# A spectral and feed-forward network on one core: the second token transform in 64x64 tiles, with other load and instruction orders

## The chip, the cores and the metric

The kernel runs on one core of a Trainium2 chip. The metric is device time in microseconds, the median of several executions. One execution was also taken by the hardware profiler; its rows are quoted below. TensorE is called PE in the rows (its weight loads PEld), VectorE DVE, ScalarE ACT, GpSimd POOL and SyncE SP. The queues from which DMAs are issued are SP, ACT and POOL.

## What is computed

One sequence of S = 2048 tokens with D = 448 features passes through two spectral layers and two feed-forward layers in turn. All is bf16, with a residual added each time.

```python
def _A_ref(x, w_r, w_i):
    X = rfft2(x.astype(float32), axes=(-2, -1))
    X = X * (w_r + 1j * w_i)                       # [2048, 225]
    return irfft2(X, s=(S, D), axes=(-2, -1)).astype(bfloat16)

def _B_ref(x, w1, b1, w2, b2):                     # 448 -> 1792 -> 448
    h = relu(x @ w1 + b1) ** 2
    return h @ w2 + b2

for _ in range(2):
    x = x + _A_ref(_layernorm(x), w_r, w_i)
    x = x + _B_ref(_layernorm(x), w1, b1, w2, b2)
```

## The kernel before

The tokens are split as s = 16 p + t: p is the partition (128), t the tile (16 tiles of 128 x 448). The token transform of 2048 points is done in two steps, one over p (128 points) and one over t (16 points with twiddle factors), and the feature transform of 448 points lies between them. The stages of a spectral layer are:

- **A1** (first layer, `first_A`, line 871) or **A2** (second, `second_A`): for each tile t the transform over p. Mean and deviation come from VectorE (`ln_stats`) or, for tiles 1, 3 and 5, from ScalarE (`act_stats`). The matrix FA, scaled by 1/deviation (`scaled`, into Fs), is the moving operand of five matmuls per tile; the tile (xin) and its mirrored copy (xr, "XR", made by POOL or ScalarE, kept in VT's place) are the stationary ones. The result is evacuated to XA.
- **TD** (`stage_TD`, line 905): the feature transform. Sixteen numbers n, most taken in pairs; the columns of one n hold 4 frequencies x 16 tiles x 2 parts. It needs XA of all sixteen tiles. It is evacuated to U (in arena).
- **B** (`stage_B`, line 933): the 16-point transform over t. Each unit m0 (eight of them, 0 to 14 by two) takes 16 matmuls on 32x32 tiles of the array: four numbers n of one group G = m0 // 4 and two row strips. So a unit needs the U of four numbers n, that is of two TD pairs. It is evacuated to EF (in arena).
- **W** (`stage_W`, line 963): VectorE multiplies EF by the spectral weights Wt, into T3 (in wide). Wt holds rows of w_r and w_i that POOL gathers with indirect DMAs by the index tile ix.
- **Bi** (`stage_Bi`, line 968): eight products v of 32 matmuls on 64-row tiles, the inverse 16-point transform, evacuated to VT. Product v needs W of the numbers 2v and 2v+1.
- **TI** and **AI** (lines 994 and 1016): the inverse feature and token transforms per tile, added to x. TI needs all eight products.

The feed-forward layer follows with layer norm and transposes (`ln_B`), h (`h_part`, `h_pairs`) and o (`o_tile`).

PSUM is evacuated by ScalarE or VectorE; which of the two takes which tile is fixed by the order.

The order is written out by hand: `ORDER` (line 136) lists for each engine the numbers of the work units in the order in which it runs them. A planner (`_Sched.schedule`, line 369) goes through these lists with estimated costs, gives PSUM banks to the tiles, and puts filler matmuls (on `ones`, `warm_mm`, line 1340) into TensorE's gaps. It adds one where the planned gap is at least 120 ns and TensorE's planned work over a recent stretch is below the share `warm_share` (0.7). Every engine runs its list in order. `emit` (line 1349) writes the waits for an instruction's semaphores straight in front of it.

In the first layer TensorE's order after A1 is TD 0a, 0b, 1, 6, 7, 3; B 1, 7, 6; TD 2, 5, 4; B 2, 3, 4, 5, 0; then the products 2, 1, 4, 3, 7, 5, 0, 6 (numbers are pairs; pair 0 is cut into two single ones, and pairs 0 and 7 of B are evacuated in halves).

The loads of x: SP issues tile 0, then ix, FA, tiles 2-3, 6-7, 10-11 and 14-15; the ACT queue issues tile 1, then 4-5, 8-9 and 12-13. After them SP issues the matrices TD, G and G0 (for B), then, once tiles 10 to 13 have their deviations, H (for Bi), TI and the other weights. POOL issues six gathers: two for the first half of Wt (16 rows per partition), two of 15 rows and two of a single row for the second half. The single one is there because the mirrored list for the last strip of partitions holds the row of frequency 0 out of line.

Of the kernel before, what the change touches and what calls it, by code (L numbers as in the profile page):

```python
# [19 lines left out]
WS = 16 * (LW + 1) + 2  # L20
# [13 lines left out]
def make_constants():  # L34
# [45 lines left out]
    G = np.zeros((P, 16, 2, 32))  # L80
    G0 = np.zeros((P, 4, 32))
    for n in range(16):
        for i in range(4):
            C, Sn = wave(16 * (n % 4) + 4 * (n // 4) + i + 1)
            a, b = pair(C, Sn), pair(Sn, -C)
            G[32 * i:32 * i + 32, n] = np.stack([np.concatenate([a, -b], 1), np.concatenate([b, a], 1)], 1)
    z = np.zeros((16, 16))
    C, Sn = wave(64)
    for k, (a, b) in enumerate(((C, -Sn), (Sn, C))):
        G0[96:128, k] = np.concatenate([pair(a, z), pair(b, z)], 1)  # L90
    C, Sn = wave(0)
    for k, (a, b) in enumerate(((C, Sn), (-Sn, C))):
        G0[96:128, 2 + k] = np.concatenate([pair(z, a), pair(z, b)], 1)

# [23 lines left out]
    ix = np.stack([P * k + 16 * j + 1, P * (16 - k) - 16 * j - 15, np.where(j == 3, P * k, P * (16 - k) - 16 * j - 16)], 1)  # L118
# [28 lines left out]
1273 1234 1240 1278 1284 1281 1287 1290""",  # L147
    "act": """
# [11 lines left out]
1049 1229 1180 1182 1177 1175 1246 1244 1251 1256 1254 1261 1249 1264 1271 1269 1259 1266 1276 1274""",  # L160
    "dve": """
# [125 lines left out]
class _Sched:  # L287
# [6 lines left out]
    DMA_FIRST = 3500.0  # L294
    TURN = 100.0
    BEGIN = 800.0
    WINDOW = 3413.0

    def __init__(self):
        self.ops = {e: [] for e in self.ENGINES}  # L300
# [300 lines left out]
def bass_interleave_layers__spectral_gfnet__dense_activation_squared_relu__prompt_kernel(nc, A_x, A_w_r, A_w_i, B_x, B_w1, B_b1, B_w2, B_b2, out):  # L601
# [7 lines left out]
    with ExitStack() as es:  # L609
# [205 lines left out]
        for w in range(2):  # L815
            gather(2, w, WS * (2 + w), 1)
# [602 lines left out]
```

## Time and profile before

| | us |
|---|---|
| median of 3 runs | 262.47 |
| range of the runs | 262.4 to 263.34 |
| the profiled execution | 263.08 |
| its span, first to last instruction | 260.9 |
| TensorE busy (share of the span) | 248.7 (95%) |
| VectorE busy | 192.8 (74%) |
| ScalarE busy | 168.4 (65%) |
| POOL busy | 15.7 (6%) |

The profiled time lies 2.2 us above its span; what is outside the span is launch and end. A busy share is an average over stages with different limits: TensorE's 95% holds the feed-forward parts, where it never stops, and the spectral parts, where it does. Matmuls are pipelined, so the busy time of a single one counts its whole passage. The rows further below are read by stretches.

### The profile page before, as it was taken

The page shows a single profiled execution, that of the slowest core. Times are in us where ns is not written, and L with a number is a line of the kernel's source. Part 1 is how long each engine was busy: PE and PEld are TensorE (multiplying, and loading weights), DVE is VectorE, ACT ScalarE, POOL GpSimd, SP SyncE. Part 2 cuts the span into 40 slices and gives each one's busy share as a digit, 9 for nine tenths or more (in the row PEclk, how much of TensorE's full clock was granted, in tenths as well). Part 3 has the DMA queues.
Part 4 walks back from the last instruction along what each step waited for, and adds up shares of the span by engine and source line. Part 5 has one row for each costly group of instructions (what it writes and reads, how often), then busy time and mean ns, then how long its engine had stood idle before and what let it go on. Part 6 is the DMA issues. An engine that isn't in the chain of part 4 may idle for free.

```text
span 260.9 us, 6550 instructions
## 1 busy us (share of the span) xinstructions
PE 248.7 (95%) x2584; PEld 155.5 (60%) x2584; DVE 192.8 (74%) x625; ACT 168.4 (65%) x362; POOL 15.7 (6%) x31
## 2 busy tenths in 40 slices
PE   8799988999999989999998997999999999999996
PEld 2478687796544445554566666899554454544454
DVE  3985976889962999969999697899993359221562
ACT  6896985999238747306937897999557794007500
POOL 6791000000000000000000000000000000000000
PEclk9999997999999999999999999999999999999999
DMA  6989662111411000110000000020352001200025
GB/s 190 405 322 346 233 190 80 23 20 40 77 43 40 4 0 0 43 41 0 3 0 4 3 3 3 3 40 5 82 69 49 3 0 40 43 0 0 3 94 187
DMA packets 23789, 17.79 MB, mean 68 GB/s; under 512 B 16142, under 2 KB 22382, under 8 KB 23760
## 3 DMA queue, kind: packets, MB, share of 16 engines
q1 hardware_dynamic: 22544, 12.90, 18.6%
q0 software_dynamic: 640, 3.69, 3.5%
q10 hardware_dynamic: 576, 0.80, 1.0%
q8 instruction: 20, 0.33, 0.5%
q14 instruction: 9, 0.07, 0.1%
HBM read 11.88 MB, written 1.84 MB: 53 GB/s over the span
## 4 chain that ended last, share of the span: by engine, by line
PE 81%; DVE 9%; ACT 6%; DMA 2%; issue 1%; SPq 0%
PE ps L705 80%; ACT arena L730 3%; DVE arena L759 2%; DMA xin<-in_A_x_dram 2%; DVE st L835 1%; DVE XA L731 1%; DVE xin L759 1%; ACT wide L730 1%; DVE wide L759 1%; ACT VT L730 1%; ACT arena L724 0%; SPq L695 0%; DVE VT L1078 0%; PE ps L1341 0%; ACT mv L724 0%
## 5 line engine op out<-in xcount | busy, mean ns | idle before, releaser
L705 PE MATMUL ps<-wide,W_sb 64*128 64x512 bf16 (+1 forms) x770 | 90.0, 346 | 0.2 <-ACT wide L730 0.2
L705 PE MATMUL ps<-W_sb,arena 128*128 128x448 bf16 (+3 forms) x476 | 86.8, 342 | 0.0
L724 ACT ACTIVATE arena<-ps,b1col 128x512 bf16<-128x512 f32 x84 | 52.8, 687 | 32.1 <-PE ps L705 31.8
L705 PEld LDWEIGHTS ps<-wide,W_sb 64*128 64x128 bf16 (+1 forms) x770 | 50.8, 95 | 36.8 <-issue 1.7
L705 PEld LDWEIGHTS ps<-W_sb,arena 128*128 128x128 bf16 x476 | 45.5, 98 | 38.1 <-DVE arena L759 0.6
L759 DVE TENSOR_TENSOR arena<-arena 128x512 bf16<-128x512 bf16 (+1 forms) x140 | 45.0, 362 | 28.0 <-ACT arena L724 27.8
L730 ACT ACTIVATE arena<-ps 128x896 bf16<-128x896 f32 (+1 forms) x28 | 20.9, 850 | 3.4 <-PE ps L705 3.1
L724 ACT ACTIVATE mv<-mv,epst 128x1 f32<-128x1 f32 (+1 forms) x45 | 12.4, 292 | 13.1 <-DVE mv L768 7.0
L1077 ACT ACTIVATE VT<-x_sb 128x448 bf16<-128x448 bf16 x28 | 16.0, 575 | 7.1 <-DVE x_sb L1053 7.1
L724 ACT ACTIVATE arena<-ps 128x256 bf16<-128x256 f32 x56 | 17.4, 394 | 1.1 <-PE ps L705 1.0
L759 DVE TENSOR_TENSOR wide<-arena,Wt 128x896 bf16<-128x896 bf16 x32 | 17.7, 620 | 0.3 <-ACT arena L730 0.2
L705 PE MATMUL ps<-H_sb,wide 64*128 64x128 bf16 x512 | 16.4, 215 | 0.7 <-ACT arena L730 0.7
L705 PEld LDWEIGHTS ps<-H_sb,wide 64*128 64x128 bf16 x512 | 15.8, 94 | 2.0 <-DVE wide L759 1.3
L730 ACT ACTIVATE wide<-ps 128x896 bf16<-128x896 f32 (+3 forms) x20 | 14.4, 759 | 3.8 <-PE ps L705 3.5
L1199 DVE SCALAR_TENSOR_TENSOR x_sb<-ps,mv,xin 128x448 bf16<-128x448 f32 (+2 forms) x13 | 8.0, 644 | 11.4 <-PE ps L705 11.3
L705 PE MATMUL ps<-wide,VT 64*128 64x512 bf16 x42 | 15.8, 376 | 0.0
L730 ACT ACTIVATE XA<-ps 128x512 bf16<-128x512 f32 (+1 forms) x28 | 14.5, 591 | 1.3 <-PE ps L705 1.3
L730 ACT ACTIVATE VT<-ps 128x1024 bf16<-128x1024 f32 (+1 forms) x16 | 12.7, 829 | 2.7 <-PE ps L705 2.5
L705 PE MATMUL ps<-TI_sb,VT 112*128 112x112 bf16 (+1 forms) x128 | 10.7, 238 | 3.6 <-DVE VT L731 1.9
L741 ACT ACTIVATE wide<-x_sb,rstd 128x448 bf16<-128x448 bf16 x10 | 6.7, 668 | 9.2 <-DMA wide<-wide 7.9
L1053 DVE SCALAR_TENSOR_TENSOR x_sb<-ps,mv,xin 128x448 bf16<-128x448 f32 x16 | 10.8, 677 | 2.4 <-PE ps L705 2.3
L731 DVE CAST arena<-ps 128x896 bf16<-128x896 f32 (+1 forms) x10 | 8.2, 853 | 5.5 <-PE ps L705 5.5
(80 smaller groups left out, 279.7 us busy)
## 6 DMA issues: line engine op xcount, KB each, us to landing
out_dram<-x_sb SPq DMA_DIRECT2D x15, 112.0 KB, 1.8
W_sb<-in_B_w_dram SPq DMA_DIRECT2D x1, 1568.0 KB, 9.2
H_sb<-c_H SPq DMA_DIRECT2D x2, 768.0 KB, 10.2
W_sb<-in_B_w_dram SPq DMA_DIRECT2D x1, 1344.0 KB, 12.8
xin<-in_A_x_dram SPq DMA_DIRECT2D x4, 224.0 KB
xin<-in_A_x_dram ACTq DMA_DIRECT2D x3, 224.0 KB, 2.9
VT<-in_B_w_dram SPq DMA_DIRECT2D x2, 192.0 KB, 3.2
G_sb<-c_G SPq DMA_DIRECT2D x1, 256.0 KB
```

Source lines behind the costliest of these rows:

```text
L705: return sch.add("pe", lambda e: e.matmul(_res(o), lhsT, rhs, start=start, stop=stop, skip_group_check=skip), [lhsT, rhs], [o], cost=cost, ...
L724: sch.add("act", lambda e: e.activation(o, _res(i), func, **kw), rd, [o], cost=c)
L730: op = sch.add(engs[0], lambda e: e.activation(o, _res(i), ACT.Copy) if h[0].eng == "act" else e.tensor_copy(o, _res(i)), [i], [o], cost=c ...
L731: e.tensor_copy(o, _res(i)), [i], [o], cost=c[engs[0]], unit=unit)
L741: op = sch.add(engs[0], lambda e: e.activation(o, i, ACT.Copy, scale=s) if h[0].eng == "act" else e.tensor_scalar(o, i, s, 1.0, op0=ALU.mu ...
L759: sch.add(eng, lambda e: e.tensor_tensor(o, _res(a), b, op), [a, b], [o], cost=_free(o) / rate + 69.0)
L835: small(lambda e, si=si, xi=xi: e.bn_stats(si, xi), [xi], [si], _free(xi) / 0.96 + 69.0)
L1053: small(lambda e, xx=xx, xi=xi, r=r, m=m: e.scalar_tensor_tensor(out=xx, in0=_res(r), scalar=m, in1=xi, op0=ALU.subtract, op1=ALU.add), [r ...
L1077: op = sch.add("act", lambda e, i=i, o=o, x=x, h=h: e.activation(o, x, ACT.Square, accum_out=sd[:, i, 1:2]) if h[0].eng == "act" else e.sc ...
L1199: small(lambda e: e.scalar_tensor_tensor(out=o, in0=_res(i), scalar=rs[0] if rs else 1.0, in1=xi, op0=ALU.add if t >= 4 and last else ALU. ...
```

## The change

Stage B now runs on 64x64 tiles of the array: a unit m0 takes the numbers n = m0 and m0 + 1 alone, on two row halves. Two 32x32 matrices stand on the diagonal of each 64x64 matrix in G (and G0), and the rest of it is zero. For this FA takes the same order of frequencies as FI. G and G0 are twice as large. Since the zeros of the last number are in another strip now, the row of frequency 0 is loaded over the first row of the last 32 partitions by two plain DMAs on SP, after H; the gathers are four, of 16 rows each. Tiles 0 to 5 of x are loaded one by one. `emit` hangs TensorE's waits, but for the latest one of an instruction, on earlier instructions that have none. The planner's model of TensorE has a pace and depth of instruction supply (`PACE`, `DEEP`), and `warm_share` is 0.8. The orders of all engines are written anew; the order lists are left out here.

In the new order of the first layer TensorE runs, after A1, TD 3, 1, 7, 2, 6; B 7, 3, 1, 6; TD 4, 0a, 0b, 5; B 2, 4, 0; products 3, 7; B 5; products 1, 4, 0, 5, 2, 6. In the second it runs TD 7, 0b, 1, 4, 2, 5; B 7, 4, 2; TD 0a; B 1; TD 3; B 0, 5; product 7; B 3; TD 6; products 4, 0; B 6; products 2, 5, 1, 3, 6 (before: TD 7, 5, 6, 4, 1, 2, 0b, 0a; B 4, 7; TD 3; B 0, 1, 6, 5, 3; products 4, 7; B 2; products 0, 5, 3, 6, 1, 2). In A1 its tiles come as 0, 5, 1, 2, 3, 6, 7, 9, 8, 4, 12, 13, 10, 11, 14, 15 (before 1, 0, 4, 2, 3, 6, 7, 8, 9, 5, 13, 12, 10, 14, 11, 15). The ACT queue issues tile 1, 5, 8-9, 3, 12-13. POOL runs: ones, XR 0, XR 1, a memset, the scaling for tile 0, a gather of the second half, XR 4-5, XR 8-9, the scaling for tile 5, XR 2-3, XR 6-7, the other gather of the second half, XR 10-11, a scaling, a gather of the first half, XR 12-13, the last gather, XR 14-15, two scalings and two memsets.

```diff
-WS = 16 * (LW + 1) + 2
+WS = 16 * (LW + 1)
...
-            FA[:, n, i] = np.stack(comps(16 * (n % 4) + 4 * (n // 4) + i + 1), 1)
-            FI[n, i] = np.stack(comps(16 * (2 * (n % 2) + i % 2) + 2 * (n // 2) + i // 2 + 1), 0)
+            kappa = 16 * (2 * (n % 2) + i % 2) + 2 * (n // 2) + i // 2 + 1
+            FA[:, n, i] = np.stack(comps(kappa), 1)
+            FI[n, i] = np.stack(comps(kappa), 0)
...
-    G = np.zeros((P, 16, 2, 32))
-    G0 = np.zeros((P, 4, 32))
+    G = np.zeros((P, 16, 2, 64))
+    G0 = np.zeros((P, 4, 64))
...
+            r, c = slice(32 * i, 32 * i + 32), slice(32 * (i % 2), 32 * (i % 2) + 32)
+            G[r, n, :, c] = np.stack([np.concatenate([a, -b], 1), np.concatenate([b, a], 1)], 1)
...
-    ix = np.stack([P * k + 16 * j + 1, P * (16 - k) - 16 * j - 15, np.where(j == 3, P * k, P * (16 - k) - 16 * j - 16)], 1)
+    ix = np.stack([P * k + 16 * j + 1, P * (16 - k) - 16 * j - 16], 1)
...
-        self.warm_share = 0.7
+        self.warm_share = 0.8
...
+        def supply(start):
+            nonlocal sent
+            sent = max(sent + self.PACE, begun[-self.DEEP])
+            start = max(start, sent)
+            begun.append(start)
+            return start
...
-            a = WS * 2 + (LW + 1) * (15 - n) + (n < 15)
+            a = WS * 2 + (LW + 1) * (15 - n)
...
-        for i, (a, n) in enumerate(((0, 1), (1, 1), (2, 2), (4, 2), (6, 2), (8, 2), (10, 2), (12, 2), (14, 2))):
-            dma("act" if i % 2 else "sp", xin[:, a:a + n, :], x_dram[:, a:a + n, :])
-            if i == 0:
+        for a, n, q in ((0, 1, "sp"), (1, 1, "act"), (2, 1, "sp"), (3, 1, "act"), (4, 1, "sp"), (5, 1, "act"), (6, 2, "sp"),
+                        (8, 2, "act"), (10, 2, "sp"), (12, 2, "act"), (14, 2, "sp")):
+            dma(q, xin[:, a:a + n, :], x_dram[:, a:a + n, :])
+            if a == 2:
+                dma("sp", FA_sb[:], dc["FA"])
+            if a == 4:
                 dma("sp", ix[:], dc["ix"])
-                dma("sp", FA_sb[:], dc["FA"])
...
         for w in range(2):
-            gather(1, w, WS * (2 + w) + LW + 2, 15)
-        for w in range(2):
-            gather(2, w, WS * (2 + w), 1)
+            gather(1, w, WS * (2 + w), 16)
...
-            u = sch.new_unit("pe", 16, "q")
-            G, i0 = m0 // 4, m0 % 4
+            u = sch.new_unit("pe", 32, "quad")
             streams = []
-            for j in range(4):
+            for j in range(2):
                 for i in range(2):
-                    n, r = 4 * G + j, slice(32 * (i0 + i), 32 * (i0 + i) + 32)
+                    n, r = m0 + j, col(i)
...
-                    o = [lambda b, i=i, j=j, c=c: ps[32 * j:32 * j + 32, b + (i if both else 0), c] for c in
+                    o = [lambda b, i=i, j=j, c=c: ps[col(j), b + (i if both else 0), c] for c in
...
+        for w, a in enumerate((A_w_r, A_w_i)):
+            sch.tag = f"L.W0.{w}"
+            dma("sp", Wt[96:128, WS * (2 + w):WS * (2 + w) + LW + 1],
+                bass.AP(a.tensor, a.offset, [[0, 2], [P * (LW + 1), 16], [1, LW + 1]]))
...
+        def spread(ops, needs):
+
+            for i, op in enumerate(ops):
+                for key in sorted(needs[i], key=lambda k: needs[i][k][1])[:-1]:
+                    for j in range(i - 1, max(i - 80, 0), -1):
+                        if ops[j] in sch.done and sch.done[ops[j]] - ops[j].cost < needs[i][key][1] + 150.0:
+                            break
+                        if not needs[j]:
+                            needs[j][key] = needs[i].pop(key)
+                            break
```

## Rows read from the trace of the kernel before

**Rows 1.** Stretches: length, then busy us (x instructions) per engine; PEclk, DMA share, GB/s.

```profile
7.10:19.20 12.10, 10.58 (x89) 7.75 (x89) 11.36 (x48) 11.45 (x31) 10.30 (x19) 1.00 0.95 364
19.20:30.00 10.80, 10.27 (x194) 7.74 (x194) 6.92 (x10) 8.33 (x13) 0.98 (x2) 1.00 1.02 352
...
38.30:40.20 1.90, 0.03 (x1) 0.01 (x1) 1.23 (x2) 1.45 (x3) 0.00 (x0) 1.00 1.10 351
40.20:47.40 7.20, 6.98 (x68) 6.04 (x69) 4.84 (x15) 4.65 (x9) 0.00 (x0) 0.76 0.07 21
47.40:141.20 93.80, 92.91 (x734) 54.24 (x735) 80.66 (x312) 57.63 (x140) 0.00 (x0) 1.00 0.11 23
...
144.60:160.75 16.15, 15.53 (x450) 12.33 (x451) 13.73 (x24) 14.70 (x20) 0.00 (x0) 1.00 0.01 3
160.75:162.85 2.10, 0.61 (x5) 0.14 (x3) 1.66 (x2) 1.35 (x2) 0.00 (x0) 1.00 0.00 0
162.85:168.40 5.55, 5.39 (x67) 4.66 (x68) 4.67 (x15) 4.93 (x10) 0.00 (x0) 1.00 0.01 3
```

**Rows 2.** Chain of waits in order of time: start us, length us, what.

```profile
16.15 2.84 DVE XA L731 x5
...
39.18 0.69 DVE VT L731
39.87 0.35 issue
...
162.72 0.14 issue
```

**Rows 3.** ScalarE in order of time, 19 to 40 us: start, length, instructions, idle before.

```profile
19.81 0.54 ACT L730 ACTIVATE arena<-ps 128x448 bf16<-128x448 f32 x1 [0.59 <-PE ps L705]
21.73 2.54 ACT L730 ACTIVATE arena<-ps 128x896 bf16<-128x896 f32 x3 [1.37 <-PE ps L705]
24.67 7.74 ACT L730 ACTIVATE arena<-ps 128x448 bf16<-128x448 f32 x11 [0.40 <-PE ps L705]
...
33.73 3.52 ACT L730 ACTIVATE VT<-ps 128x1024 bf16<-128x1024 f32 x4 [0.41 <-PE ps L705]
38.07 1.72 ACT L730 ACTIVATE VT<-ps 128x512 bf16<-128x512 f32 x3 [0.82 <-PE ps L705]
```

**Rows 4.** Groups of instructions, shapes apart: busy us, mean ns, idle before.

```profile
L730 ACT ACTIVATE arena<-ps 128x448 bf16<-128x448 f32 x7 | 3.8, 570 | 1.0 <-PE ps L705 1.0
L705 PE MATMUL ps<-arena,G_sb 32*32 32x448 bf16 x252 | 7.5, 352 | 0.4 <-ACT arena L730 0.2
```

**Rows 5.** TensorE in order of time around stage B, both spectral parts.

```profile
22.38 0.94 PE L705 MATMUL ps<-TD_sb,XA 128*128 128x224 bf16 x8
23.25 1.33 PE L705 MATMUL ps<-arena,G_sb 32*32 32x448 bf16 x50
...
154.07 0.57 PE L705 MATMUL ps<-arena,G_sb 32*32 32x448 bf16 x16
154.61 0.60 PE L705 MATMUL ps<-H_sb,wide 64*128 64x128 bf16 x15
```

**Rows 6.** The start: a landing (chain of waits), POOL and TensorE in order of time.

```profile
2.12 5.47 DMA xin<-in_A_x_dram
...
7.55 1.02 POOL L806 DMA_INDIRECT Wt<-in_A_w_i_dram,ix  x1 [0.18 <-issue]
9.00 0.48 POOL L742 TENSOR_SCALAR Fs<-FA_sb,rstd 128x256 bf16<-128x256 bf16 x1 [0.43 <-DVE rstd L866]
9.44 0.55 POOL L731 COPY VT<-xin 128x448 bf16<-128x448 bf16 x1
...
12.28 0.27 PE L705 MATMUL ps<-Fs,xin 128*128 128x256 bf16 x1
...
15.33 1.03 POOL L806 DMA_INDIRECT Wt<-in_A_w_r_dram,ix  x1
...
18.58 0.22 PE L705 MATMUL ps<-Fs,m 128*128 128x128 bf16 x1
```

More of the change, by code (lines that the diff above doesn't have):

```diff
@@ L78, in pair @@
         return np.stack([a, b], 1).reshape(32, 16)
-    G = np.zeros((P, 16, 2, 32))
-    G0 = np.zeros((P, 4, 32))
+    G = np.zeros((P, 16, 2, 64))
+    G0 = np.zeros((P, 4, 64))
     for n in range(16):
         for i in range(4):
-            C, Sn = wave(16 * (n % 4) + 4 * (n // 4) + i + 1)
+            C, Sn = wave(16 * (2 * (n % 2) + i % 2) + 2 * (n // 2) + i // 2 + 1)
             a, b = pair(C, Sn), pair(Sn, -C)
-            G[32 * i:32 * i + 32, n] = np.stack([np.concatenate([a, -b], 1), np.concatenate([b, a], 1)], 1)
+            r, c = slice(32 * i, 32 * i + 32), slice(32 * (i % 2), 32 * (i % 2) + 32)
+            G[r, n, :, c] = np.stack([np.concatenate([a, -b], 1), np.concatenate([b, a], 1)], 1)
+            if n == 15 and i == 2:
+                G0[r, 0::2, c], G0[r, 1::2, c] = G[r, n, 0:1, c], G[r, n, 1:2, c]
     z = np.zeros((16, 16))
@@ L89, in make_constants @@
     for k, (a, b) in enumerate(((C, -Sn), (Sn, C))):
-        G0[96:128, k] = np.concatenate([pair(a, z), pair(b, z)], 1)
+        G0[96:128, k, 32:64] = np.concatenate([pair(a, z), pair(b, z)], 1)
     C, Sn = wave(0)
     for k, (a, b) in enumerate(((C, Sn), (-Sn, C))):
-        G0[96:128, 2 + k] = np.concatenate([pair(z, a), pair(z, b)], 1)
+        G0[96:128, 2 + k, 32:64] = np.concatenate([pair(z, a), pair(z, b)], 1)
     H = np.zeros((P, 16, 2, 3, 16, 2, 2))
@@ L297 @@
     WINDOW = 3413.0
+    PACE = 34.15
+    DEEP = 24
     def __init__(self):
@@ L397, in schedule @@
         done = {}
+        begun = [0.0] * self.DEEP
+        sent = 0.0
+        def supply(start):
[4 more added lines that the diff above has]
+            return start
         left = {u: len(npred[u]) for u in self.units}
@@ L543, in schedule @@
             for op in u.ops:
-                t += op.cost
+                t = (supply(t) if e == "pe" else t) + op.cost
                 done[op] = t
@@ L702, in mm @@
                 cost *= unit.rows / 128.0
-            if unit is not None and unit.mode == "q":
-                cost = max(cost, 21.0)
             return sch.add("pe", lambda e: e.matmul(_res(o), lhsT, rhs, start=start, stop=stop, skip_group_check=skip),
@@ L936, in stage_B @@
             t = [_Tile(2)] * 2 if both else [_Tile(1), _Tile(1)]
[L937 to L938 removed]
+            u = sch.new_unit("pe", 32, "quad")
             streams = []
[L940 removed]
+            for j in range(2):
                 for i in range(2):
[L942 removed]
+                    n, r = m0 + j, col(i)
                     x = U[r, n, :]
                     xs = x.rearrange("p (r l) -> p r l", r=2)[:, ::-1]
[L945 removed]
+                    o = [lambda b, i=i, j=j, c=c: ps[col(j), b + (i if both else 0), c] for c in
                          (slice(0, 2 * LW), slice(0, LW), slice(LW, 2 * LW))]
[L947 to L948 removed]
+                    if n < 15 or i == 0:
+                        s_ = [(t[i], o[0], G_sb[r, n, 0, :], x), (t[i], o[0], G_sb[r, n, 1, :], xs)]
                     else:
[L950 removed]
+                        s_ = [(t[i], o[1 + k // 2], G0_sb[r, k, :], x[:, LW:] if k in (1, 2) else x[:, :LW]) for k in range(4)]
                     streams.append(s_)
@@ L1347, in bass_interleave_layers__spectral_gfnet__dense_activation_squared_relu__prompt_kernel @@
         sch.assign_tickets()
-        def emit(ename, eng):
-            waited = {}
-            def need(key, t):
-                if waited.get(key, 0) < t:
-                    eng.wait_ge(sem[key], t)
-                    waited[key] = t
-            for op in sch.ops[ename]:
-                for dop in op.deps:
-                    need(dop.semkey(), dop.ticket)
-                if op.is_dma and op.ticket > 16:
-                    need(op.semkey(), op.ticket - 16)
+        def spread(ops, needs):
[7 more added lines that the diff above has]
+                            break
+        def emit(ename, eng):
+            ops, waited, needs = sch.ops[ename], {}, []
+            for op in ops:
+                n = {}
+                for key, t, at in [(d.semkey(), d.ticket, sch.done.get(d, 0.0) + d.lat) for d in op.deps] + (
+                        [(op.semkey(), op.ticket - 16, 0.0)] if op.is_dma and op.ticket > 16 else []):
+                    if waited.get(key, 0) < t:
+                        waited[key] = t
+                        n[key] = (t, at)
+                needs.append(n)
+            if ename == "pe":
+                spread(ops, needs)
+            for op, n in zip(ops, needs):
+                for key, (t, at) in n.items():
+                    eng.wait_ge(sem[key], t)
                 ins = op.fn(eng)
@@ L1366, in emit @@
                     ins.then_inc(sem[(ename, False)], 1)
-            last = {op.dsem: i for i, op in enumerate(sch.ops[ename]) if op.is_dma}
+            last = {op.dsem: i for i, op in enumerate(ops) if op.is_dma}
             for j in sorted(last, key=last.get):
-                need((ename, True, j), sch.final[(ename, True, j)])
+                if waited.get((ename, True, j), 0) < sch.final[(ename, True, j)]:
+                    eng.wait_ge(sem[(ename, True, j)], sch.final[(ename, True, j)])
         with nc.Block() as block:
```

26 lines of the change are left out of this document (13 added, 13 removed), and 84 rows, old and new, of the table ORDER.

## The prediction

> **What bounds the kernel now.** I read the stretches first, to see which engine is full where [rows 1]. The reader is to see two kinds. In the feed-forward parts (47.40 to 141.20, and likewise the last 90 us) TensorE is busy 92.91 of 93.80 us: nothing of the change touches that work. In the spectral parts no engine is full for long and the others wait for each other in turn, so those parts (7 to 47 and 141 to 168 us) hold all that can be won. Then the chain of waits in order of time [rows 2], to see what ends each barrier: the first transform of x ends with VectorE's evacuations, which run to 18.99; the first spectral part ends with the evacuations of VT, after which TensorE starts TI at 40.22. Third, ScalarE alone over 19 to 40 us [rows 3]: it works from 19.81 to 39.79 with four waits for TensorE (1.37 + 0.40 + 0.41 + 0.82 = 3.00 us), so 16.98 us of work in a stretch of 19.98. That is the engine whose work reaches to the end of the stretch. In the second spectral part ScalarE is busy 14.70 of 16.15 us, TensorE 15.53 [rows 1].
>
> Last, the clock: from 40.20 to 47.40 the granted clock is 0.76 of 2.4 GHz on average, the only stretch below 1.00. Before it TensorE had 0.03 us of work in the 1.90 us from 38.30. At the same place of the second spectral part it had 0.61 us of filler work in 2.10 and then 1.5 us of nothing, and the clock stayed at 1.00 [rows 1].
>
> **The change, part by part.** The profiled execution took 263.08 us, its span 260.9 us; the median of the runs is 262.47. The sum is made against 263.08 and then carried to the median.
>
> *Stage B in 64x64 tiles.* Per transform 130 matmuls of 32x32 become 66 of 64x64. Work on the array is the same: 448 columns, 16 matmuls on 8 tiles at a time before, 8 on 4 now, two rounds each. The row: 50 matmuls, a little over three units, in 1.33 us including the length of the last [rows 5], some 0.40 us a unit; two rounds of 448 columns at 2.4 GHz are 0.37 us. So the tiles by themselves win at most 0.03 us x 16 units = 0.5 us on TensorE, none of it on ScalarE; I take nothing. What counts is that a unit now needs only the one TD pair of its own number, where it needed two. The order can then alternate TD and B, and products (Bi) start before the last B.
>
> *First spectral part.* ScalarE's list, counted from the old and new order: ten evacuations of 896 columns in both, four of 1024, four of 512, but four instead of five of 448. By the rows [rows 4] one of 448 costs 3.8 / 7 = 0.54 us, so 16.98 - 0.54 = 16.4 us of work remain. It starts later: the first pair on ScalarE is now the second one on TensorE, 16 matmuls at about 0.10 us (eight in 0.94 with the last one's length [rows 5]) after 19.2 plus some 0.2 us to the evacuation, 21.0 instead of 19.81; but the wait of 1.37 us after a lone first evacuation is gone with that. With the other three waits kept (1.63 us) it ends at 21.0 + 16.4 + 1.6 = 39.0, and TI follows at 39.2: -1.0 us. The ends: no waits at all gives 37.6 (-2.6), all 3.00 us of waits 40.6 (+0.4). I take -1.0, since two of the three waits are for the last products, which still wait for VectorE's multiplications.
>
> *Waits spread.* Before TI 0.35 us passed from the last evacuation to the first matmul; in the second part 0.14 us [rows 2]. The difference is the extra wait instructions that are now hung on earlier ones. It lies within the 0.2 us that I left after 39.0. Elsewhere TensorE runs ahead of its data or is covered; from 0 to -0.5 us, I take 0. A wait moved forward holds all matmuls queued behind it, and with them both evacuating engines, if its engine is late against the plan; it is moved mostly by an instruction or two, so +0.2 us is the other end.
>
> *The clock before the first feed-forward part.* In the new order ScalarE holds one whole and one half VT evacuation at the end instead of three halves (1.72 us of them in the old, from 38.07 [rows 3]), so the idle time before TI should be 1.0 to 1.2 us (last product, half an evacuation of 1.72 / 3, about 0.6, the wait), shorter than the 1.5 us that left the clock at 1.00; the raised filler share also lets fillers into shorter gaps. The same work took 7.20 us at 0.76 and 5.55 us at 1.00 [rows 1], so up to -1.65; 7.20 x 0.24 = 1.73 is the loss by the clock itself. I take -1.4, as a quicker TensorE will wait a little for the evacuations that it has outrun. Ends 0 and -1.7.
>
> *Start, loads in single tiles.* No fewer bytes come earlier: before, four tiles were requested ahead of FA on the two queues, now too (0, 1, 2, 5). FA keeps its third place on SP, so the first matmul stays at about 7.1. The second tile on TensorE is now 5, whose scaling stands on POOL behind one gather and two copies. The gather waits for ix, now fifth on SP; the fourth request there landed at 7.60 before [rows 6]. From 7.6: gather 1.02, two copies of 0.55, scaling 0.48, so 10.2, TensorE at 10.3. Behind tile 5 wait fourteen others, in order. In the old run tile six started at 12.28 and the last matmul at 18.58 [rows 6]: 11 tiles at 0.58 with their waits. Fifteen of them from 10.3 end at 19.0, so +0.3. VectorE gets four scalings more and one evacuation less. Ends: -0.6 (the waits inside those 11 tiles gone: five matmuls of 256 columns at 2.4 GHz are 0.53 us, so some 0.5 us are waits) and +1.6 (twice those waits, and a landing 1 us later). I take +0.3. Fewer gathers save two POOL issues of 1.0 us; these lay after POOL's other work. The two new loads on SP, behind H, must wait until the gathers whose first row they overwrite have landed; queued behind them are TI, FI, J, the biases, W1, TQ and W2, first read from 40 us on, and those gathers are now the first two of POOL's four, so I expect no wait. The last gather is then issued near 15 as before (15.33 [rows 6]), and VectorE first needs it for its multiplications near 24; G grows by 288 KB, under 1 us of transfer at the 352 to 364 GB/s that this stretch moves [rows 1], read first at 23.25 [rows 5].
>
> *Second spectral part.* ScalarE's list has the same counts in both orders, so no gain is taken; ends -0.5 and +0.9 (two halves of the last XA now on VectorE in a row, and the switches below). Order of the feed-forward parts: 0.
>
> Sum: +0.3 - 1.0 - 1.4 = -2.1 us: 261.0 for a profiled execution like this one, 262.47 - 2.1 = **260.4 us** at the median.
>
> [...] Between two products one B unit took 154.07 to 154.61, 0.54 us for about 0.39 us of work [rows 5]: two changes of tile shape and one wait in 0.15 us, so under 0.1 us each. The new orders hold seven more such changes (6 against 4 in the first transform, 11 against 6 in the second), 0.7 us, in the shade of ScalarE. [...]
>
> **The rivals.** (1) The clock falls again before TI, because the idle time does not shrink under the old 1.9 us: only +0.3 - 1.0, **261.8**. For it: the barrier stays; against: fewer evacuations at its end. 0.17. (2) The first spectral part is not shorter, since the products wait for sixteen multiplications on VectorE in either order and ScalarE keeps its 3 us of waits; the clock falls too: +0.3, **262.8**. 0.09. (3) Each of seven more changes of shape costs the 0.35 us that a matmul of 448 columns lasts [rows 4], uncovered: +2.5 on the forecast, **262.9**. 0.05. (4) Slower: tile 5 in second place holds TensorE. It decides from 10.3 on: 15 tiles at 0.55 to 0.58 then just reach the old end, and each further 1 us goes to TD, which needs all sixteen tiles, and on to TI. If the copy of tiles 4 and 5 (tile 4 sits behind FA on SP) and the scaling come at 12.7, that is +2.4, and with the plan for the fillers broken the clock is not won: 0.3 + 2.4 - 1.0 = +1.7, **264.2**. For it: POOL's line is sequential and DMA is busy 0.95 of that stretch; against: the gathers, which before ran among the loads, now come after them. 0.14. That the change doesn't do what it says can hardly be: stage B is rewritten whole.
>
> **How the numbers follow.** Forecast 0.55. Its own range, with the ends combined, is 257.9 to 261.7. The range to 264.0 takes in rivals 1 to 3 and most of 4, leaving out under 2 in 10. A measurement of this kernel can tell 0.5% (1.3 us) from no change. Faster than 261.2: nine tenths of the forecast and a quarter of rival 1, 0.54. Slower than 263.8: rival 4 and a little of 2 and 3, 0.16. Within: 0.30.
>
> **What would show it.** TI's first matmul near 39.2 and the granted clock at 1.00 behind it; ScalarE with about 16.4 us of work up to there; first matmul of stage TD near 19.5; B units at 0.4 us; second spectral part as long as before; feed-forward parts unchanged. Wrong if the clock falls again, if TensorE's second tile comes after 10.4, or if ScalarE's waits in 19 to 39 stay at 3 us.

## The result and the profile after

The changed kernel takes 258.6 us at the median of its executions (258.13, 258.32, 258.87 and one of 263.36 whose mean clock was only 0.987, left out of the ratio), against 262.71 for the kernel before in the same comparison: a ratio of 0.9834, with a 95% interval of 0.9803 to 0.9865, so some 4.4 us less. I had forecast 260.4 with 257.9 to 264.0 around it: the sign and the range hold, the size was half of what came; the time lies at the low end of the range. The profiled execution took 258.13 us, its span 256.3.

First the stretches of the kernel after, which answer to [rows 1] (same columns; cut at the first matmuls of stages A1, TD, TI, h, second TD, second TI, second h, and the last matmul's end):

```profile
6.53:19.22 12.69, 11.43 (x93) 8.16 (x94) 12.33 (x51) 11.83 (x32) 10.18 (x17) 1.00 0.99 350
19.22:39.60 20.38, 18.35 (x389) 15.13 (x390) 15.54 (x24) 16.44 (x23) 0.00 (x0) 1.00 0.83 273
39.60:45.50 5.90, 5.87 (x77) 5.08 (x77) 5.01 (x15) 5.04 (x9) 0.00 (x0) 1.00 0.29 89
45.50:140.88 95.38, 95.17 (x756) 56.02 (x754) 82.93 (x325) 61.00 (x147) 0.00 (x0) 1.00 0.12 23
140.88:158.06 17.18, 15.88 (x391) 12.20 (x389) 15.67 (x27) 15.85 (x21) 0.00 (x0) 1.00 0.01 3
158.06:164.52 6.46, 6.24 (x85) 5.55 (x84) 5.61 (x17) 5.62 (x11) 0.00 (x0) 1.00 0.01 3
164.52:253.97 89.45, 89.37 (x672) 50.72 (x668) 53.73 (x160) 47.57 (x112) 0.00 (x0) 1.00 0.20 44
```

The same cuts in the profiled executions of all kernels of this study give the table on which the experiments rest (us; FF1 is from TI to the second TD, FF2 from the second TI to the last matmul's end; clock is the granted clock of the stretch from TI to h; in no_spread and h_later it fell before TI, see 5 and 8):

```
kernel            to TD   TD to TI   FF1     TD to TI   FF2    clock
                          (first)            (second)
before            19.23   20.99     104.37   18.26     95.69   0.76
after             19.22   20.38     101.28   17.18     95.91   1.00
no_spread         19.54   23.35     101.38   17.08     95.77   1.00
ffn0_old          19.65   21.25     103.00   17.18     95.76   1.00
s2_old            19.69   20.74     101.28   17.71     95.77   1.00
s1_old            19.39   20.48     101.31   17.19     95.75   1.00
share07           18.75   20.71     101.28   17.08     95.77   1.00
before_share08    19.06   20.93     102.76   18.27     95.68   1.00
before_ffn0_new   19.86   21.38     103.26   18.27     95.69   0.78
tiles_loads       19.63   20.73     102.32   17.78     95.69   1.00
h_later           19.41   23.93     101.27   17.19     95.75   1.00
w1_later          19.26   20.07     101.36   17.18     95.80   1.00
h_w1_later        19.29   20.10     101.91   17.19     95.75   1.00
s1_old_loads      19.46   19.94     101.32   17.18     95.76   1.00
```

From before to after: 0.0 up to TD, -0.6 in the first spectral part, -3.1 in the first feed-forward part, -1.1 in the second spectral part, +0.2 in the last: -4.6, which is the difference of the spans (260.9 and 256.3). Most of it came in a part that I had taken at nothing but for the clock.

The place of that gain is seen on TensorE in order of time. The kernel before, ahead of the inverse transform of tile 12:

```profile
92.77 1.46 PE L705 MATMUL ps<-wide,W_sb 64*128 64x512 bf16 x12
95.10 0.54 PE L705 MATMUL ps<-wide,FI_sb 128*128 128x224 bf16 x4 [0.87 <-DVE arena L759]
```

and the kernel after at the same place:

```profile
90.44 1.47 PE L721 MATMUL ps<-wide,W_sb 64*128 64x512 bf16 x12
91.85 0.94 PE L721 MATMUL ps<-wide,FI_sb 128*128 128x224 bf16 x8
```

The idle 0.87 us is gone, and two inverse transforms run in a row. The chain of waits of after, 10 to 40 us:

```profile
10.16 5.10 PE ps L721 x45
15.26 10.32 DMA Wt<-in_A_w_r_dram,ix
...
33.40 0.38 issue
33.78 3.75 PE ps L721 x127
37.52 0.25 issue
37.78 0.99 PE ps L721 x13
38.77 0.69 DVE VT L747
```

Two things stand in it that [rows 2] does not have: the last gather, which lands at 25.58 us and holds VectorE for 1.22 us (the one issued at 15.33 us in the kernel before landed at 24.84), and stops of TensorE named issue between products. ScalarE, which answers to [rows 3]:

```profile
20.95 1.73 ACT L746 ACTIVATE arena<-ps 128x896 bf16<-128x896 f32 x2 [1.65 <-PE ps L721]
23.25 5.07 ACT L746 ACTIVATE arena<-ps 128x896 bf16<-128x896 f32 x7 [0.57 <-PE ps L721]
28.59 2.60 ACT L746 ACTIVATE arena<-ps 128x896 bf16<-128x896 f32 x4 [0.26 <-PE ps L721]
31.53 1.09 ACT L746 ACTIVATE VT<-ps 128x512 bf16<-128x512 f32 x2 [0.34 <-PE ps L721]
32.50 0.92 ACT L746 ACTIVATE arena<-ps 128x896 bf16<-128x896 f32 x1
33.30 3.73 ACT L746 ACTIVATE VT<-ps 128x1024 bf16<-128x1024 f32 x4
37.70 1.69 ACT L746 ACTIVATE VT<-ps 128x1024 bf16<-128x1024 f32 x2 [0.68 <-PE ps L721]
```

It starts at 20.95 (forecast 21.0) and has 16.44 us of work (forecast 16.4); its waits after the start are 1.85 us (0.57 + 0.26 + 0.34 + 0.68; forecast 1.63). TI comes at 39.60 (forecast 39.2).

### The profile page after: what moved, and what is told of

The parts are those of the page before. It is cut to its first block, busy times and chain, and to the rows that moved or that the text cites. A ratio compares the mean times of both kernels' runs of the same rounds, so it can differ in the third digit from the quotient of the medians.

```text
span 256.3 us, 6151 instructions
## 1 busy us (share of the span) xinstructions
PE 247.0 (96%) x2462; PEld 154.4 (60%) x2462; DVE 193.3 (75%) x628; ACT 167.2 (65%) x362; POOL 12.5 (5%) x26
## 4 chain that ended last, share of the span: by engine, by line
PE 82%; DMA 7%; ACT 4%; DVE 3%; issue 1%; POOL 1%; SPq 0%; DVEq 0%; POOLq 0%
PE ps L721 81%; DMA Wt<-in_A_w_r_dram,ix 4%; ACT arena L746 2%; DMA FA_sb<-c_FA 2%; DMA wide<-wide 2%; ACT wide L746 1%; DVE wide L775 1%; ACT VT L746 1%; DVE x_sb L1214 1%; PE ps L1361 0%; POOL Wt L824 0%; DVE arena L747 0%; POOL Fs L758 0%; DVE st L851 0%; SPq L713 0%
## 5 line engine op out<-in xcount | busy, mean ns | idle before, releaser
L721 PEld LDWEIGHTS ps<-wide,W_sb 64*128 64x128 bf16 (+1 forms) x770 | 51.4, 95 | 36.1 <-DMA wide<-wide 0.9
L740 ACT ACTIVATE arena<-ps,b1col 128x512 bf16<-128x512 f32 x84 | 51.9, 691 | 29.1 <-PE ps L721 28.8
L775 DVE TENSOR_TENSOR arena<-arena 128x512 bf16<-128x512 bf16 (+1 forms) x140 | 44.0, 362 | 29.7 <-ACT arena L740 29.7
L746 ACT ACTIVATE XA<-ps 128x512 bf16<-128x512 f32 (+1 forms) x28 | 15.3, 596 | 3.3 <-PE ps L721 3.3
L721 PEld LDWEIGHTS ps<-H_sb,wide 64*128 64x128 bf16 x512 | 14.4, 94 | 3.3 <-issue 1.6
L746 ACT ACTIVATE VT<-ps 128x512 bf16<-128x512 f32 (+1 forms) x16 | 12.6, 822 | 1.7 <-PE ps L721 1.4
L1361 PE MATMUL ps<-ones 128*128 128x512 bf16 (+2 forms) x32 | 10.1, 437 | 2.8 <-ACT VT L746 1.1
L757 ACT ACTIVATE wide<-x_sb,rstd 128x448 bf16<-128x448 bf16 x12 | 7.8, 665 | 6.3 <-DVE mv L784 6.0
L747 DVE CAST arena<-ps 128x448 bf16<-128x448 f32 (+1 forms) x11 | 8.8, 831 | 3.2 <-PE ps L721 3.2
L1068 DVE SCALAR_TENSOR_TENSOR x_sb<-ps,mv,xin 128x448 bf16<-128x448 f32 x16 | 10.3, 676 | 0.8 <-PE ps L721 0.7
```

The costliest lines, as they stand in the source:

```text
L721: return sch.add("pe", lambda e: e.matmul(_res(o), lhsT, rhs, start=start, stop=stop, skip_group_check=skip), [lhsT, rhs], [o], cost=cost, ...
L740: sch.add("act", lambda e: e.activation(o, _res(i), func, **kw), rd, [o], cost=c)
L746: op = sch.add(engs[0], lambda e: e.activation(o, _res(i), ACT.Copy) if h[0].eng == "act" else e.tensor_copy(o, _res(i)), [i], [o], cost=c ...
L747: e.tensor_copy(o, _res(i)), [i], [o], cost=c[engs[0]], unit=unit)
L757: op = sch.add(engs[0], lambda e: e.activation(o, i, ACT.Copy, scale=s) if h[0].eng == "act" else e.tensor_scalar(o, i, s, 1.0, op0=ALU.mu ...
L775: sch.add(eng, lambda e: e.tensor_tensor(o, _res(a), b, op), [a, b], [o], cost=_free(o) / rate + 69.0)
```

## The experiments

Where a kernel has an old order for a part, the lists of TensorE, ScalarE and VectorE for that part stand in the order of the kernel before, numbers shifted by the two added units; SP's list of loads and stores stays that of the changed kernel. Ratios are against the kernel before in the same comparison.

**1. Order of the first feed-forward part: ffn0_old.**

```diff
 ORDER["pe"], stage names in place of the numbers, around 92 us (act and dve likewise):
-AI0.12 AI0.14 o0.6 o0.4 o0.7 o0.5
+AI0.12 o0.7 AI0.14 o0.6 o0.4 o0.5
```

> The changed kernel with the old order of its first feed-forward part on TensorE, ScalarE and VectorE (everything from TI to the last transposition of the normalized output tiles); all else of the change stays. Theory A (the 1.6 us won there come from the new order: the old one lets TensorE wait 1.1 us near 94 us for a bank that ScalarE has not emptied): 259.6 to 260.2, a gap of about 1 us on TensorE ahead of an FI product near 91 to 93 us. Rival B (they come from the spread waits, the earlier start or the fillers, the order is neutral): 258.2 to 258.7, no such gap.

Measured: 260.66 us, ratio 0.9915 (0.9879 to 0.9950). FF1 is 103.00 instead of 101.28. TensorE there:

```profile
92.66 1.46 PE L721 MATMUL ps<-wide,W_sb 64*128 64x512 bf16 x12
94.05 0.61 PE L1361 MATMUL ps<-ones 128*128 128x512 bf16 x2
94.89 0.56 PE L721 MATMUL ps<-wide,FI_sb 128*128 128x224 bf16 x4 [0.24 <-ACT arena L740]
```

The wait is back, now filled in part by two fillers, and ScalarE's evacuation ends it. With everything else of the change in place the old order costs 1.7 us of stretch, so theory A holds and B falls. The median is some 2.3 us above the changed kernel's, a little above A's range; in the profiled execution the rest lies ahead of TI, where the part from TD took 21.25 us instead of 20.38.

**2. The same from the other side: before_ffn0_new.** The kernel before with the new order in that part alone.

> The kernel before with the new order of its first feed-forward part alone (the change undone everywhere else). Theory A (the new order by itself removes the wait of 1.1 us near 94 us and some small ones): 1.4 to 1.8 us below the kernel before, 260.8 to 261.3, and 95.2 to 95.6 us from h to the second TD at the same clock. Rival B (it needs the earlier start or the spread waits): 262.3 to 262.9.

Measured: 261.93 us, ratio 0.9964 (0.9925 to 1.0003); h to the second TD 95.67 us against 97.17. The kernel before, then this one:

```profile
47.42:144.59 97.17, 95.24 (x761) 55.73 (x761) 83.31 (x327) 60.72 (x146) 0.00 (x0) 1.00 0.11 23
48.83:144.50 95.67, 94.73 (x753) 55.87 (x753) 83.38 (x325) 60.85 (x147) 0.00 (x0) 1.00 0.11 23
```

The stretch is A's, the median of all executions is not, because the clock fell in 7 of its 10 and in 7 of the 19 that it is compared with. At equal clock it is 262.05 against 263.45 us (0.993) and 260.74 against 261.70 (1.00), so 1.0 to 1.4 us less, at A's lower end or a little under it.

**3. Order of the second spectral part: s2_old.**

```diff
 ORDER, units of TD1.* to the last product: TD, B and products as in the kernel before
```

> The changed kernel with the old order of the second spectral part alone; the 64x64 tiles stay. Theory A (the gain of 1.1 us there is the order that the finer dependency allows, TD and B in turn): 259.3 to 259.7, 18.1 to 18.4 us from TD's first matmul to TI's. Rival B (it is the tiles of 64x64 themselves, or the waits spread): 258.2 to 258.6, 17.1 to 17.3 us.

Measured: 259.19 us, ratio 0.9871 (0.9816 to 0.9927), 17.71 us of stretch:

```profile
141.71:159.42 17.71, 16.03 (x392) 12.61 (x390) 15.76 (x27) 15.94 (x21) 0.00 (x0) 1.00 0.01 3
```

Between both theories: of the 1.08 us, half (18.26 to 17.71) comes with the 64x64 tiles in the old order, half (17.71 to 17.18) with the order. The run with tiles and loads alone (7) has 17.78 there and says the same. TensorE's last product ended 16.23 us after TD's first matmul before, 15.76 us after it here and 15.58 in the changed kernel. So the tiles end TensorE's work earlier, and of what the order adds, 0.35 us is a shorter barrier behind it (1.95 to 1.60).

**4. Order of the first spectral part: s1_old.**

> The changed kernel with the old order of the first spectral part alone; 64x64 tiles, loads, fillers' rule and the waits spread stay. Theory A (the new order is worth 0.6 us up to TI and the shorter idle time before TI keeps the clock): TI's first matmul at 40.2 or later, granted clock from TI to h near 0.76, 259.9 to 260.8 in all. Rival B (the order matters little because the last gather, landing at 25.6, holds VectorE in either order; the clock is kept by the fillers): TI's first matmul within 0.3 us of 39.6, clock at 1.00, 258.2 to 258.8.

Measured: 258.19 us, ratio 0.9842 (0.9785 to 0.9899); TI at 39.87, clock 1.00. B holds: the new order on which I had built -1.0 us gives 0.1 us of stretch and nothing at the median.

**5. Waits spread: no_spread.**

```diff
-            if ename == "pe":
-                spread(ops, needs)
```

> The changed kernel (258.4 us) without the step that moves waits to earlier instructions of TensorE; order, tiles, loads and fillers stay. Theory A (the spread is worth about nothing, as I took it; 0 to 0.5 us): 258.4 to 258.9, TI's first matmul at 39.6 to 39.9 and the first feed-forward part as long as now. Rival B (the spread is what shortened the second spectral part and the first feed-forward part, 1.1 + 1.6 us): 260.5 to 261.1, with the stretches between TD of the second part and TI, and between h and the second TD, back at their old lengths.

Measured: 258.62 us, ratio 0.9844 (0.9789 to 0.9899). A holds for the time and for the first feed-forward part (101.38 us). TI can't be read from the profiled execution: at 261.27 us it is the only one of five with a mean clock below 1.00. The last gather landed only at 27.8 us, TensorE then stood idle for 2.49 us, the clock behind fell (0.93 over the part), and TI came at 42.89:

```profile
30.08 2.10 PE L721 MATMUL ps<-arena,G_sb 64*64 64x448 bf16 x24 [2.49 <-DVE arena L747]
19.54:42.89 23.35, 19.77 (x389) 16.33 (x390) 15.64 (x24) 16.38 (x23) 0.00 (x0) 0.93 0.81 259
```

Over the eight traces with these loads the gather lands at 25.2 to 27.8 us.

**6. What keeps the clock: before_share08 and share07.**

```diff
-        self.warm_share = 0.7
+        self.warm_share = 0.8
```

> The kernel before with the new filler share of 0.8 alone. Its own executions show two times, 261.1 at a mean clock of 1.000 and 262.6 to 263.6 at 0.993. Theory A (shorter idle time by tiles and order keeps the clock; the share by itself does little): 262.0 to 262.9 and still both clocks. Rival B (the share keeps the clock): all executions near 261.1 with a mean clock of 1.000.

Measured: 261.51 us, ratio 0.9977 (0.9945 to 1.0009), all ten executions at a mean clock of 1.000. The stretches before and after TI:

```profile
38.04:39.99 1.95, 0.61 (x5) 0.14 (x3) 1.26 (x2) 1.49 (x3) 0.00 (x0) 1.00 1.09 342
39.99:45.57 5.58, 5.45 (x68) 4.75 (x69) 4.51 (x15) 4.67 (x9) 0.00 (x0) 1.00 0.07 18
```

Here 0.61 us of filler stand in the 1.95 us before TI; in [rows 1] the 1.90 us held 0.03 us, and the clock behind was 0.76. B holds on the kernel before. Over the four comparisons of these experiments the kernel before ran 51 times: 25 executions at a mean clock of 1.00 (median 261.5 us) and 26 at 0.993 (median 263.3). So the clock is worth 1.8 us, but only in half of the executions.

> The changed kernel with the old filler share of 0.7 (fillers are put into idle time of TensorE only where the planned activity is below that share); all else stays. Theory A (the idle time before TI has become short enough by the tiles and the order; the share only adds to it): granted clock 1.00 in all stretches, 258.2 to 258.8. Rival B (the fillers keep the clock): after TI the clock falls to about 0.76 in most executions, 259.6 to 260.2.

Measured: 258.08 us, ratio 0.9845 (0.9787 to 0.9904), clock 0.999 to 1.000 in its four executions: A holds, 0.1 us below its range. Without a filler TensorE's idle time before TI is 1.41 us, against 1.89 in the kernel before:

```profile
39.46 1.32 PE L721 MATMUL ps<-TI_sb,VT 112*128 112x224 bf16 x16 [1.41 <-DVE VT L747]
```

So under the new orders the old share keeps the clock too. Either one keeps it; the next run shows that the tiles alone do not.

**7. Tiles and loads alone: tiles_loads.** Old order on TensorE, ScalarE and VectorE from the first spectral part to the end, no spreading, share 0.7.

> Only the 64x64 tiles, the loads in single tiles and the four gathers of the change: from TI's spectral part on to the end the old order stands on TensorE, ScalarE and VectorE, waits are not spread, the filler share is the old 0.7. Theory A (what the single runs gave: new order of the first feed-forward part -1.7, of the second spectral part -0.5, order of the first spectral part and spread 0, tiles in the second part -0.5, and the shorter first part keeps the clock): 260.3 to 261.2, clock 1.00 after TI. Rival B (tiles and loads leave the idle time before TI as it was, so the clock falls in some executions): the executions split, some at 0.993 with 261.8 to 262.8. Rival C (the parts need each other, the tiles with the old order are worth nothing): 262 or more at a clock of 1.00.

Measured: 262.27 us, ratio 1.0000 (0.9959 to 1.0040); mean clock 1.00 in four of ten executions (261.4 to 262.3), 0.993 to 0.998 in six. Rival B holds for the clock. The total looks like C's, but it holds a cost of the edit itself: SP's list of output stores stayed in the new order, while VectorE finishes the last tiles in the old one. SP waits for one tile until 254.2 us and has nine stores left then:

```profile
254.22 4.58 SPq L713 DMA_DIRECT2D out_dram<-x_sb  x9
```

So the span ends 4.27 us after the last matmul, against 2.34 to 2.37 us in the other thirteen traces. The last matmul itself ends at 256.15 us, 0.55 us earlier than in before_share08 (256.70), whose clock is 1.00 too. Without those 1.9 us the median would be near 260.4, an estimate from this one trace and inside A's range; so C is not shown, and the total says nothing against the sum of the single runs. The tiles' gain in the second spectral part is there (17.78 against 18.26). The first part, with a stop of TensorE among the products that the kernel before does not have, ends no earlier (TI at 40.35). The chain of waits:

```profile
28.48 4.54 PE ps L721 x133
33.02 1.32 issue
34.34 5.23 PE ps L721 x147
```

**8. The last gather: h_later.** (Only the argument that changes is shown, with comments; likewise in 9.)

```diff
-after=[rstd[:, 10 + 2 * i, 0:1]])     # both loads of H
+after=[Wt[:, WS:WS + 1]])             # ... wait for the third gather
```

> The changed kernel with the two loads of H released not by the statistics of tiles 10 and 12 (issued at 15.95 us, against the last gather) but by the landing of the third gather. Theory A (the last gather, landing at 25.2 to 27.8 us, holds VectorE's multiplications and through them the first spectral part): it lands at 21.5 to 23.5, TI's first matmul moves from 39.6 to 38.4 to 38.8, 257.2 to 257.7 in all, with less spread between executions. Rival B (ScalarE's work of 16.4 us sets the end in any case): gather earlier, TI at 39.4 to 39.7, 258.2 to 258.6. Rival C (H now lands after the first products want it at 29.1): TI at 40 or later, 259 or more.

Measured: 259.0 us, ratio 0.9882 (0.9823 to 0.9940). The gather landed at 22.58 and VectorE's multiplications began at 24.67 without a wait, as A said; yet TI came at 43.34. TensorE:

```profile
36.16 5.82 PE L721 MATMUL ps<-H_sb,wide 64*128 64x128 bf16 x144 [2.70 <-issue]
41.91 0.61 PE L1361 MATMUL ps<-ones 128*128 128x512 bf16 x2
```

The total is C's, its cause is not: H had landed at 26.8 and 28.6 us. None of the theories had what these lines show: a stop of 2.70 us that no engine and no load of the kernel ends, after which the clock fell (0.93 over the stretch) and 144 products took 5.82 us. (The profiled execution, 261.71 us, is the only one of the five with a mean clock below 1.00; the others took 258.92 to 259.49.) The DMA records show what it goes with. On a queue named instruction come packets of 16 KB, 19 in the changed kernel's trace for TensorE's 4924 recorded matmuls and weight loads, so one for about 259 of them. In seven traces TensorE stops ahead of the same instruction, and it goes on a nearly constant time after the end of the second such packet behind TD's start:

```
kernel       packet begins   ends     TensorE goes on   difference
after            30.94       32.26         33.78            1.52
s1_old           30.97       32.46         34.01            1.55
s2_old           31.83       33.11         34.61            1.50
ffn0_old         32.45       33.48         35.07            1.59
share07          30.71       32.16         33.70            1.54
tiles_loads      31.51       32.89         34.34            1.45
h_later          33.54       34.62         36.16            1.54
```

In each the packet stands among the loads of H, TI and W1. In the kernel before the same packet ended at 30.08, and TensorE reached that instruction at 31.47, 1.39 us later, so without a stop. In no_spread, slowed by the clock, it came there 3.4 us after the packet's end and did not stop either. The stops lasted 0.2 (share07) to 2.7 us (h_later). That such a packet holds the instructions with which TensorE goes on is my reading of the queue's name, the count and these times; no row shows what is in it.

**9. W1 out of the way: w1_later.**

```diff
         spectral(True)
+        for k in _pages(VT[:, 0, 0, 0, 64:65]):          # evacuation of product 4
+            sch.units[159].ops[0].deps.append(sch.last_write[k])    # load of W1
+            sch.units[159].ops[0].gdeps.append(sch.last_write[k])
```

> The changed kernel with the load of W1 (1.5 MB, now running from 28 to 33 us) released only by the evacuation of the product numbered 4, near 34 us; all else stays. Theory A (TensorE stops before a product at 33 us, named issue, because a 16-KB packet of its instructions begins only at 30.9 us behind the loads; in seven traces it goes on 1.53 us after that packet ends): without W1 beside it the packet begins near 28 to 29.5, the stop of 0.4 to 2.7 us at 33 to 36 us is gone, TI's first matmul at 38.6 to 39.4, 257.6 to 258.2. Rival B (the stop is something else, or the multiplications on VectorE behind the last gather hold the stretch anyway): 258.2 to 258.7, TI at 39.5 to 40.5.

TQ and W2, queued on SP behind W1, move with it. Measured: 257.45 us (257.17 to 257.82), ratio 0.9780 (0.9735 to 0.9825), a little below A's range. The packet begins at 29.13, ends at 30.00, and TensorE:

```profile
29.27 1.96 PE L721 MATMUL ps<-H_sb,wide 64*128 64x128 bf16 x64
31.16 0.57 PE L721 MATMUL ps<-arena,G_sb 64*64 64x448 bf16 x8
31.67 5.99 PE L721 MATMUL ps<-H_sb,wide 64*128 64x128 bf16 x192
37.59 0.61 PE L1364 MATMUL ps<-ones 128*128 128x512 bf16 x2
```

The stops are gone, as A said, and TI comes at 39.33; the part from TD to TI is 0.3 us shorter (20.07 against 20.38). The median is 0.9 us below the changed kernel's 258.32 (its three executions at a clock near 1.00), but in another comparison, and the intervals of the two ratios overlap; more than the 0.3 us of the trace is not shown.

**10. Both loads moved, new and old order: h_w1_later, s1_old_loads.** Edits 8 and 9 together; in the second also the old order of the first spectral part.

> Both loads moved: H released by the third gather, as in the run where the last gather landed at 22.6 us and TensorE then stopped for 2.7 us, and W1 released by the evacuation of product 4. Theory A (gather and code packets were the two things that kept the first spectral part at 20.4 us): both waits are gone, TI's first matmul at 37.8 to 38.6, clock 1.00, 256.8 to 257.5 in all, under both kernels. Rival B (ScalarE's 16.4 us and the products set the end): TI at 39 to 39.6, 258.0 to 258.6.

> As the run with both loads moved, but with the old order of the first spectral part. Theory A (the new order's gain of about 1 us, which I forecast, was there but hidden by the last gather and the code packet): TI's first matmul 0.6 to 1.2 us later than in the run with the new order, 257.6 to 258.4. Rival B (the order of this part is worth nothing in any case): within 0.3 us of that run.

Measured: 258.45 us, ratio 0.9828 (0.9782 to 0.9873), and 257.84, ratio 0.9798 (0.9754 to 0.9843). TI comes at 39.39 in both, whatever the order: B holds in both for TI; the totals differ by the 0.6 us that h_w1_later loses behind TI, where its chain has a transposing DMA of 4.56 us. The gather is early in both (23.7 and 22.4 us) and the stops are gone, so the two together were worth 0.3 us of the part with the new order (20.38 to 20.10) and 0.5 with the old (20.48 to 19.94), and do not bound what is left of it. What is left shows on TensorE with the old order:

```profile
28.31 1.33 PE L721 MATMUL ps<-arena,G_sb 64*64 64x448 bf16 x24 [0.28 <-DVE arena L747]
29.63 8.10 PE L721 MATMUL ps<-H_sb,wide 64*128 64x128 bf16 x256
```

These are 256 products without a gap, 31.6 ns each. The kernel before has the same; below it its whole part from TD to TI, columns as in [rows 1]:

```profile
30.05 8.28 PE L705 MATMUL ps<-H_sb,wide 64*128 64x128 bf16 x256 [0.33 <-ACT arena L730]
19.23:40.22 20.99, 18.52 (x450) 15.63 (x451) 15.11 (x23) 16.77 (x23) 0.95 (x2) 1.00 0.81 262
```

TensorE is busy 18.52 us there and ScalarE 16.77, and neither order moves TI. So TensorE's own work and the barrier behind it bound this part as far as these runs show; no run made that work shorter.

## Why the prediction was right in sign and half in size

- **Start, +0.3; 0.0 came:** TensorE's second tile came at 10.16 (forecast 10.3), TD at 19.22 (19.5; before 19.23). Over the eleven traces with the new loads TD starts at 18.75 to 19.69, over the three with the old ones at 19.06 to 19.86: nothing either way. The fourth rival, decided from 10.3 to 10.4 on, missed by 0.15 us in this execution, and that was luck: over the eleven traces the second tile came at 9.69 to 10.69, in four of them after 10.4, at a cost to TD of under 0.5 us.
- **First spectral part, -1.0; -0.6 came, by another way.** The failed step is to take as bound ScalarE because "that is the engine whose work reaches to the end of the stretch". Its work and its start were forecast to 0.1 us, but its waits for TensorE are TensorE's own work, and that is the longer of the two (18.52 against 16.77 us, experiment 10). In the kernel before, products run from 30.05 to 38.33 without a gap; after, they start 0.9 us earlier (29.14) and lose that to a B unit that now stands among them (0.5 us) and to the two stops named issue (0.38 + 0.25; TensorE goes on from the second at 37.78, 1.43 us after the third packet, 35.47 to 36.35, has ended). What was won is the barrier, from 38.33 to TI: 1.89 us before, 1.27 after, close to the 1.0 to 1.2 I gave.
- **The last gather:** the forecast gave its issue (near 15; 15.26 came) and the time at which VectorE needs it (near 24), but no landing. It landed 10.32 us after its issue, beside the loads of H, and held VectorE 1.22 us. That cost little, since TensorE's products ended the part; in the execution where it landed at 27.8, TI was 3 us late, in part by the clock. The "no wait" of the forecast, which is for the two new loads on SP, held: they were issued at 16.79 and 17.66, and the gathers before them had landed at 13.46 and 16.59.
- **Clock, -1.4:** in the profile 104.37 to 102.76 us with the share alone, -1.6; right in size and place. What I did not see: the profiled execution was one of the half that lose the clock. Against the median the term is worth about half, 0.9 us. And the reason was only half right: by experiment 6 fillers keep it on the kernel before (ten of ten executions), and so does the shorter idle time of the new orders without them (four of four).
- **Order of the feed-forward parts, 0; -1.5 to -1.7 came** (experiments 1 and 2). This is the largest miss. I read 92.91 of 93.80 us busy and let the remaining 0.89 go as out of reach, without asking what it was: nearly all of it is the one wait of 0.87 us ahead of tile 12's inverse transform. So it is not true that TensorE never stops in the feed-forward parts. (From the matmul group before it to that transform 2.33 us passed before and 1.41 after; the barrier at the end of the part gives 0.2 to 0.4 more; the last few tenths the traces don't single out.) "Nothing of the change touches that work" was wrong, since the orders of all engines there were new.
- **Second spectral part, 0; -1.1 came.** Mis-sized twice: the tiles themselves, "at most 0.5 us, I take nothing", gave 0.5 by experiment 3, since there too TensorE (15.53 of 16.15 us in [rows 1]) and not ScalarE (14.70) was the fuller engine. About half of that came ahead of the last 192 products and half in them (6.21 us before, 5.97 in s2_old), and why these got shorter is open. The alternating order gave 0.5 more.
- **Waits spread, 0:** right (experiment 5). The 0.35 us ahead of TI, which I put down to extra wait instructions, is 0.14 in the changed kernel and 0.15 in no_spread, where every wait stands straight in front of its instruction; so they are not shown to be its cause.
- **The range:** how 257.9 to 261.7 follows from the ends is not worked out; added in squares they give -2.0 and +2.5 us, so 258.4 to 262.9. The measured time lies at that lower end, so it is in the stated range by little.
- **Changes of tile shape:** one B unit between two products takes 0.5 us in the new kernel as well (31.16 to 31.67 in experiment 9), and in the second spectral part the order with more changes of shape is the faster one (17.18 against 17.71 us, experiment 3). No run shows the third rival's 0.35 us for each change.

The sum is right in sign because the clock term and a little of the first part were there; it was short by the 2.6 us of two stretches in which I had named the wrong engine or had not asked. For the median the parts add up to some 0.9 (clock) + 0.6 + 1.5 + 1.1 = 4.1 us of the 4.4 measured, an estimate from these runs.

## What to carry to other kernels

Where an engine is 99% busy over a long stretch, look up the one wait that makes up the rest before calling an edit of the order neutral; and take as bound the engine whose own work, added up without its waits, is longest, not the one that happens to work last. When a stop ends at no engine and no load, look at the packets of the queue named instruction in the DMA records, and try large loads that are needed late in another place than the stretches in which an engine runs through its instructions fastest (0.3 us of stretch here). A time taken from one execution should first be placed among the others: half of the gain by the clock was not there at the median. And where an order is put back for an experiment, put back every engine's list, SP's stores too: 1.9 us of one total came from a list left behind.

## What the runs showed of the hardware

At a granted clock of 1.00 the trace of the kernel before has 42 matmuls of 448 columns from 186.05 to 194.00 us, 0.189 us each, and 40 of 256 columns from 174.83 to 179.20, 0.109 us each: 0.417 ns for each column more, 2.4 columns per ns, which is what the forecast's 2.4 GHz stands for. On the queue named instruction the second 16-KB packet behind TD's start took 0.9 to 1.5 us. Counted from the instruction 256 before the one at which TensorE is held, it began 0.3 us later where few loads ran (w1_later; DMA share 0.18 from 28.0 to 38.2 us, against 0.64 in the changed kernel), 2.3 us later in the changed kernel and 5.4 us later in h_later, where the loads of H, TI and W1 ran. TensorE went on 1.45 to 1.59 us after the packet's end in every trace in which it was held there. One gather, issued at 14.8 to 15.7 us in every kernel with the new loads, landed at 25.2 to 27.8 us with H beside it and at 22.4 to 23.7 with H behind. Executions of one and the same program, the kernel before, had a mean granted clock of 1.00 in 25 of 51 cases and of 0.993 in 26; in the profiled one of the lower kind the fall stands behind a barrier in which TensorE had stood idle for 1.9 us (0.76 over the 7.2 us after it).
